# Attention with split heads and a shrink MLP: the first tile transposed in fp32, ranks computed behind tile 1, flags by another ring, copies on ScalarE

## The chip, the cores and the metric

The kernel runs on one core of a Trainium2 chip. The core has TensorE (matmuls, written PE in the profile, with its weight loads as PEld), VectorE (DVE), ScalarE (ACT), GpSimd (POOL) and SyncE (SP). SP, ScalarE and GpSimd can issue DMA transfers. All engines run in parallel, each executes its own queue in order, and they wait for each other by semaphores. The metric is the device time of one execution in microseconds (us). Lower is better.

## The reference

```python
def _attn_ref(q, k, v, is_retrieval, n_sink, window):     # q, k, v: 4 x 8 heads x 768 x 64, fp32
    scores = scale * np.matmul(q, k.transpose(0, 1, 3, 2))
    causal = rel >= 0
    stream_keep = causal & (is_sink | in_win)             # first 4 keys, or the last 64
    mask = np.where(retr[0, :, 0, 0, None, None], full_mask, stream_mask)
    ...                                                   # softmax of the masked scores
    return np.matmul(a, v)

def _moe_ref(x, w_in, w_out):                             # x: 3072 x 512, w_in 512 x 2048, w_out 2048 x 512
    h = x @ w_in
    g = h - np.tanh(h)
    return g @ w_out
```

Each of the 8 heads is either a retrieval head (causal attention over all keys) or a streaming head (the first 4 keys and a window of 64). The flags `is_retrieval` say which; 3 of 8 are set. The heads of a token side by side make the 512 columns of x.

## The kernel before, in words

**Tiles and units.** The 3072 tokens are cut into 12 tiles of 256 tokens; three tiles make one batch entry. A tile has four attention units, one for each pair of heads, so unit n belongs to tile n // 4. A unit goes through: T (TensorE transposes of q and k, `st_T`, and copies of the results from PSUM into `qT` and `kz`), S (scores, exp on ScalarE, mask product on VectorE, `st_S`), A (product with v, then a reciprocal and a product on VectorE that give x, `st_A`), X (TensorE transposes x, and a copy puts it into `xT`, `st_X`). When a tile has its four units, H units multiply xT with w_in into a `ph` bank, ScalarE takes tanh, VectorE makes `gt` (L1110), and O groups multiply gt with w_out. There are two `ph` banks, two banks pairs ("sc") shared by scores and transposes, and one bank each for A and O.

**Loads.** SP loads q, k and v in fp32 into six raw tiles used in turn (L297), so the raw q tile of tile 0 is used again by tile 2. Tile 0 is loaded in halves of four heads. The weights are loaded by GpSimd with a cast (L309, L321). Before anything else SP loads the flags (L344).

**Casts.** For tile 0 ScalarE casts three halves of q and k to fp16, VectorE the fourth (`cast_qk`, L566 and L568). GpSimd casts v. For tile 1 ScalarE casts q and k, for tile 2 GpSimd does.

**Ranks.** From tile 3 on (the second batch entry) the heads are taken in an order in which retrieval heads come first, so that the other half can use cheaper near scores. `by_rank` computes this order on VectorE by some 17 small operations, each of which uses the one before (L464 to L547), loads it into registers of GpSimd and VectorE (L553), and makes the thresholds `thrr` from which `masks` builds the masks of the ranked tiles. GpSimd then casts q, k and v of tile 3 and later by rank (`cast_ranked`, L627), and DMA transposes on SP take the place of T and X (L644, L1043). `load_count` (L1289) loads the number of set flags into a register of all five engines; after the last tile it decides whether the program must be run again without ranks (with more than 4 set flags; here it isn't).

**Order.** The program is written as a list of operations with the engine, an assumed duration, what is read and written, and optionally another operation that must come before (`after`). A planner (`Plan.run`) plays these through with the assumed durations: each engine takes, of what is ready, the operation that stands first in the list. The order found is written into the engines' queues and is fixed then. `slot` and the plan after it say between which H units the steps of the next tile's units stand in the list. In the list `by_rank` stands ahead of the first H unit, and the planner issues it as soon as VectorE is free and the flags are there. The count's load waits, in the planner's view, for the count alone.

Of the kernel before, what the change touches and what calls it, by code (L numbers as in the profile page):

```python
# [149 lines left out]
def kernel(  # L150
# [63 lines left out]
    ones = const.tile([128, 128], FP16, name="ones")  # L214
    warm = const.tile([128, 1], FP32, name="warm")
    ident16 = const.tile([128, 128], FP16, name="ident16")
    A4 = const.tile([128, 4, 128], FP16, name="A4")
    sinks = const.tile([128, 128], FP16, name="sinks")
    nz = const.tile([128, 2 * H], FP32, name="nz")
# [29 lines left out]
    def program(first):  # L249
# [90 lines left out]

        if first:
            op(
                "SP", 400,
                lambda: nc.sync.dma_start(  # L344
                    out=retr_i[:], in_=is_retrieval.bitcast(I32).partition_broadcast(128)
                ),
                w=["retr"], dma=(128, 20.0),
            )
# [3 lines left out]
        if first:  # L352

            op("POOL", 204, lambda: nc.gpsimd.memset(ones[:], 1.0), w=["ones"])
            op(
                "ACT", 1400,
                lambda: nc.scalar.activation(out=warm[:], in_=ones[:, 0:1], func=AF.Exp),
                r=["ones"], w=["warm"],
            )

            if fast:
                op(
                    "POOL", 300,
                    lambda: nc.gpsimd.affine_select(
                        out=upto[:], in_=ones[:, 0 : H * H].rearrange("p (a c) -> p a c", a=H),
                        compare_op=ALU.is_ge, fill=0.0, base=0, pattern=[[1, H], [-1, H]],
                        channel_multiplier=0,
                    ),
                    r=["ones"], w=["upto"],
                )  # L370

            def select(m, src, fill, base, step, mult, key, cmp=ALU.is_ge):
                op(
                    "POOL", 300,
                    lambda: nc.gpsimd.affine_select(
                        out=m, in_=src, compare_op=cmp, fill=fill,
                        base=base, pattern=[[step, 128]], channel_multiplier=mult,
                    ),
                    r=["ones", key], w=[key],
                )  # L380


            select(ident16[:], ones[:], 0.0, 0, 1, -1, "ident", ALU.is_equal)
            select(A4[:, 2, :], ones[:], 0.5, window_i - 1, -1, 1, "A4")
            select(sinks[:], ones[:], 0.5, n_sink_i - 1, 0, -1, "sinks")
            op(
                "DVE", 220,
                lambda: nc.vector.tensor_max(out=A4[:, 0, :], in0=A4[:, 2, :], in1=sinks[:]),
                r=["A4", "sinks"], w=["A40"],
            )  # L390
            select(A4[:, 2, :], A4[:, 2, :], 0.0, 0, 1, -1, "A4")
            select(A4[:, 3, :], ones[:], 0.5, -(128 - window_i + 1), -1, 1, "A43")
            op(
                "DVE", 220,
                lambda: nc.vector.tensor_max(out=A4[:, 1, :], in0=A4[:, 3, :], in1=sinks[:]),
                r=["A43", "sinks"], w=["A41"],
            )
# [29 lines left out]
            def make_rflag0():  # L427

                nc.vector.scalar_tensor_tensor(
                    out=rflag0[:], in0=sinks[:, 0:1].to_broadcast([128, H]), scalar=0.75,  # L430
                    in1=rflag[:], op0=ALU.is_ge, op1=ALU.max,
                )

            op("DVE", 165, make_rflag0, r=["sinks", "rflag"], w=["rflag0"])
# [19 lines left out]
        def ranked(t):  # L454
            return first and fast and t >= NG

        def by_rank():

            def dve(ns, fn, r, w):
                op("DVE", ns, fn, r=r, w=w)  # L460

            one = iota[:].unsqueeze(1).to_broadcast([128, H, H])
            dve(
# [76 lines left out]
                    out=mS[:].rearrange("p a c -> p (a c)")[:, 0:384], in0=A[:, 0:384],  # L540
                    scalar1=0.75, scalar2=None, op0=ALU.is_ge,
                ),
                r=["A4", "A40", "A41", "A43"], w=["mS"], port=True,
            )
            op(
                "DVE", 150,
                lambda: nc.vector.tensor_copy(out=mS[:, 4, :], in_=mS[:, 2, :]),  # L547
                r=["mS3"], w=["mS"], port=True,
            )
            for e, et in (("POOL", Engine.Pool), ("DVE", Engine.DVE)):  # L550

# [43 lines left out]
        def cast_ranked(t):  # L595
# [39 lines left out]
            for nm in "kq":  # L635
                for i in range(NB):
                    c0 = (g * NB + i) * KS

                    def turn(nm=nm, i=i, c0=c0):
# [8 lines left out]
                    op(  # L648
                        "SP", 1250, turn,
                        r=[key for half in range(2) for key in t16_keys(nm, t, half)],  # L650
                        w=[("kz", b % 2, g, i) if nm == "k" else ("qT", t, "all", i)],
                        dma=(128 * (8 if nm == "k" else 4), 22.0),
                    )
            if g == 0:
                for p_ in range(HP // 2):

                    def repeat(p_=p_):
# [8 lines left out]

                    hp = 2 * p_ + 1
                    op(
                        "POOL", 580, repeat, r=[("kz", b % 2, 0, 0)],
                        w=[("sinks", b % 2, hp)], port=True,  # L670
                    )

# [5 lines left out]
        def k_keys(t, hp, g):  # L678
            s = t // NG % 2
            if ranked(t):  # L680
                return [("kz", s, g, i) for i in range(NB)]
            return [("kz", s, hp, g)]

        def q_of(t, hp):
# [91 lines left out]
        def st_T(n, eq="DVE", ek=("DVE", "DVE")):  # L776
            t, hp = divmod(n, HP)
            b, g = divmod(t, NG)
            tp, key = bank([128, 2, 8, 128], FP16, "sc", f"tp{n}")
            keys = [(*key, x) for x in range(2)]  # L780
            if hp == 0:
                qT[t] = lazy(qt_pool, [128, HP, TT], FP16, "qT", f"qT{t}")
            cq, ck = t16s["q", t], t16s["k", t]

            def mm():
                for x, c in enumerate((cq, ck)):
                    for i in range(NB):
                        nc.tensor.transpose(
                            out=tp()[:, x, i, :], in_=c()[:, i, 2 * hp : 2 * hp + 2, :],
                            identity=ident16[:],  # L790
                        )

            op(
                "PE", 224, mm,
                r=["ident"] + [
                    key for nm in "qk" for key in t16_keys(nm, t, hp * 2 // HP)
                ],
                w=keys,
            )

            cost = {"ACT": 373, "DVE": 288}
            kk = kz[b % 2][:, 2 * hp : 2 * hp + 2, :]
# [380 lines left out]
        def slot(n):  # L1183
# [4 lines left out]
                res.append(qs.pop(0))  # L1188
            by_tile = ranked(n // HP)
            if n % HP and not by_tile:  # L1190
                res.append(lambda: st_X(n - 1))
            res.append(lambda: st_A(n, 0))
            if qs:
                res.append(qs.pop(0))
            res.append(lambda: st_A(n, 1))
            res += qs
            if n + 2 < NU and not ranked((n + 2) // HP):
                res.append(lambda: st_T(n + 2))
            if n % HP == HP - 1:
                if by_tile:  # L1200
                    res.append(lambda: st_X_tile(n // HP))
                else:
                    res.append(lambda: st_X(n))
            return res

        for b in range(2):
            ones_v(b)
        cast_qk(0, (("ACT", "ACT"), ("ACT", "DVE")), (0,))
        load(1, halves=range(2))
        for n in (0, 1):  # L1210
            st_T(n, "ACT", ("DVE", "DVE"))
            for f in scores(n):
                f()
        cast_v(0, ("POOL", "POOL"), (0,))
        cast_qk(0, (("ACT", "ACT"), ("DVE", "DVE")), (1,))
        for n in (0, 1):
            st_A(n, 0)
            st_A(n, 1)
# [18 lines left out]
        if first:  # L1237
            for j in range(4):
                load_w_out(j, [("win", 3)])
            if not fast:  # L1240
                for hp in range(HP):
                    zero_kz("POOL", 1, hp, 0, S, [("wout", 3)])
            if fast:
                by_rank()


        PIECES = (
# [10 lines left out]
        for t in range(1, NTT):  # L1258
# [4 lines left out]
            for hp in range(HP):  # L1263
                if t + 2 < NTT:
# [3 lines left out]
                        )  # L1268
                        for nm, i in PIECES[hp]
                    ]  # L1270
                if first and fast and t == NG - 1 and hp == HP - 1:
                    fs.append(lambda: masks(thrr, "thrr", NGEN))
                if hp == 0 and t + 1 < NTT:
                    if ranked(t + 1):
                        fs.append(lambda t=t: cast_ranked(t + 1))
                        fs.append(lambda t=t: spread_v(t + 1))
# [8 lines left out]
        if first and fast:  # L1285

            def load_count():
# [5 lines left out]
                )  # L1293

            plan[6 * NFU] = plan.get(6 * NFU, []) + [
                lambda: op("DVE", 400, load_count, r=["count"])
            ]

        def expect_skip(after, *engines):
# [71 lines left out]
```

## Time and profile before

| | |
|---|---|
| median of 5 runs | 251.59 us (250.66 to 252.67) |
| profiled execution | 251.74 us, its span 250.0 us |
| TensorE busy | 227.0 us, 91% of the span |
| VectorE, ScalarE, GpSimd busy | 151.0, 143.2, 96.4 us |
| DMA | 39.25 MB, mean 157 GB/s |

The profile shows one execution. A line of the timeline or of the groups names the engine, the line of the kernel, the operation and what it writes from what; brackets hold the idle time of the engine before it and what ended that time. The page cuts the span into 40 slices, with a digit for the tenths of it that an engine was busy. Queue entries with a q (SPq, ACTq) are what an engine's sequencer does itself, such as issuing a DMA or loading a register.

### The profile page before, as it was taken

How to read it: one execution, taken by the hardware profiler on the slowest of the kernel's cores; microseconds unless marked ns; L12 is line 12 of the kernel's file. 1: busy time of each engine (PE TensorE's matmuls, PEld its weight loads, DVE VectorE, ACT ScalarE, POOL GpSimd, SP SyncE). 2: the span in 40 equal slices, each digit the busy share in tenths (PEclk: the TensorE clock that was granted, in tenths of full speed). 3: DMA queues.
4: the chain of work that ended last, by engine and by line, in shares of the span. 5: the costliest groups of instructions: out<-in, count | busy, mean ns of one | idle time of the engine just before them, and what ended most of it. 6: DMA issues, size and time to landing. Idle time of an engine off the chain costs nothing. (4 is left out here: it accounts for less than half of the span.)

```text
span 250.0 us, 6087 instructions
## 1 busy us (share of the span) xinstructions
PE 227.0 (91%) x2204; PEld 167.0 (67%) x2204; DVE 151.0 (60%) x375; ACT 143.2 (57%) x215; POOL 96.4 (39%) x286
## 2 busy tenths in 40 slices
PE   0259999999999899999999899999999999999992
PEld 0146876786677578776777577776777777666661
DVE  7686786774468637666686555567676454643410
ACT  3357864876367539655386555547667566433430
POOL 5146080139954815937447088364340000000000
PEclk9999999999999999999999999999999999999999
DMA  5999999999979989999899999998981211041121
GB/s 124 209 201 195 197 211 188 221 204 215 201 152 210 160 173 239 184 245 194 165 210 197 184 213 153 232 138 172 220 164 64 51 45 42 5 84 42 45 81 52
DMA packets 121667, 39.25 MB, mean 157 GB/s; under 512 B 114336, under 2 KB 118688, under 8 KB 121632
## 3 DMA queue, kind: packets, MB, share of 16 engines
q1 hardware_dynamic: 117264, 34.49, 71.2%
q0 software_dynamic: 4224, 4.19, 10.1%
q8 instruction: 18, 0.29, 0.5%
q14 instruction: 17, 0.14, 0.2%
q10 hardware_dynamic: 144, 0.13, 0.2%
HBM read 27.27 MB, written 6.29 MB: 134 GB/s over the span
## 5 line engine op out<-in xcount | busy, mean ns | idle before, releaser
L1090 PE MATMUL ph<-xT,win 128*128 128x256 f16 x768 | 99.0, 273 | 1.2 <-DVE gt L1110 0.7
L1149 PE MATMUL po<-wout,gt 128*128 128x512 f16 (+1 forms) x400 | 98.1, 370 | 0.9 <-ACT ot L1125 0.9
L1110 DVE SCALAR_TENSOR_TENSOR gt<-th,ph 128x512 f16<-128x512 f32 x96 | 65.8, 685 | 53.4 <-ACT th L1103 53.2
L1103 ACT ACTIVATE th<-ph 128x512 f32<-128x512 f32 x96 | 57.4, 598 | 64.9 <-PE ph L1090 62.9
L1090 PEld LDWEIGHTS <-win 128*128 128x128 f16 x768 | 72.2, 98 | 16.8 <-issue 1.2
L936 ACT ACTIVATE pt<-sc 128x768 f16<-128x768 f32 (+1 forms) x60 | 53.9, 917 | 16.1 <-PE sc L918 15.6
L1149 PEld LDWEIGHTS <-gt 128*128 128x128 f16 x400 | 36.7, 98 | 24.0 <-issue 1.3
L918 PE MATMUL sc<-qT,kz 128*128 128x256 f16 (+1 forms) x280 | 34.7, 259 | 5.2 <-DVE kz L774 3.2
L985 PEld LDWEIGHTS <-pt 128*128 128x128 f16 x552 | 26.4, 99 | 12.0 <-DVE pt L949 2.0
L627 POOL CAST k<-raw_k 128x128 f16 x72 | 20.0, 321 | 31.6 <-DMA raw_k<-in_k_dram 24.9
L918 PEld LDWEIGHTS <-kz 128*128 128x128 f16 x280 | 24.2, 102 | 11.5 <-DVE kz L774 3.7
L985 PE MATMUL av<-v,pt 128*128 128x65 f16 x304 | 26.0, 198 | 1.5 <-DVE pt L949 1.5
L627 POOL CAST t_q<-raw_q 128x128 f16 x72 | 19.7, 313 | 16.9 <-DMA raw_q<-in_q_dram 16.5
L1015 DVE TENSOR_TENSOR x16t<-av,rinv 128x128 f32 x72 | 20.9, 290 | 2.2
L627 POOL CAST v<-raw_v 128x128 f16 x72 | 19.3, 312 | 6.0 <-DMA raw_v<-in_v_dram 5.9
L985 PE MATMUL av<-vf,pt 128*128 128x65 f16 x248 | 20.0, 193 | 0.5 <-ACT pt L936 0.5
L875 ACT ACTIVATE pt<-sc 128x1024 f16<-128x1024 f32 (+1 forms) x18 | 17.2, 954 | 4.2 <-PE sc L861 3.3
L1125 ACT ACTIVATE ot<-po 128x512 f32<-128x512 f32 (+1 forms) x24 | 14.2, 593 | 9.0 <-PE po L1149 8.7
L954 DVE TENSOR_TENSOR pt<-pt,m 128x1024 f16<-128x1024 f16 x20 | 14.5, 726 | 4.2 <-ACT pt L936 3.9
L1005 DVE RECIPROCAL rinv<-av 128x4 f32<-128x4 f32 x48 | 8.6, 179 | 12.6 <-PE av L985 11.9
L892 DVE TENSOR_TENSOR pt<-pt,mS 128x512 f16<-128x512 f16 x24 | 10.7, 485 | 6.7 <-ACT pt L875 6.7
L568 POOL CAST v<-raw_v 128x512 f16<-128x512 f32 x6 | 4.0, 673 | 19.2 <-DMA raw_v<-in_v_dram 16.2
(71 smaller groups left out, 122.4 us busy)
## 6 DMA issues: line engine op xcount, KB each, us to landing
out_dram<-ot SPq DMA_DIRECT2D x23, 256.0 KB, 2.5
raw_q<-in_q_dram SPq DMA_DIRECT2D x20, 256.0 KB, 4.6
raw_k<-in_k_dram SPq DMA_DIRECT2D x20, 256.0 KB, 4.2
raw_v<-in_v_dram SPq DMA_DIRECT2D x20, 256.0 KB, 5.0
win<-in_moe_w_in_dram POOLq DMA_DIRECT2D x4, 512.0 KB, 10.2
wout<-in_moe_w_out_dram POOLq DMA_DIRECT2D x4, 512.0 KB, 11.7
raw_q<-in_q_dram SPq DMA_DIRECT2D x8, 128.0 KB, 3.2
raw_k<-in_k_dram SPq DMA_DIRECT2D x8, 128.0 KB, 3.3
```

Of the source, the lines that this page charges most:

```text
L627: nc.gpsimd.tensor_copy(out=o, in_=r()[:, :, at, :])
L875: lambda: nc.scalar.activation(out=pt()[:, :, 0:wid], in_=sc()[:, :, 0:wid], func=AF.Exp, scale=inv_sqrt_d),
L918: nc.tensor.matmul(out=sc()[:, hh, o : o + nb * 128], lhsT=kk[:, hh, jb * KS : jb * KS + 128], rhs=q_of(t, hp)[:, q0 * 128 : (q0 + nb) * 128],
L936: lambda: nc.scalar.activation(out=pt()[:, :, 512 * gi : 512 * gi + wid], in_=sc()[:, :, 0:wid], func=AF.Exp, scale=inv_sqrt_d,),
L954: nc.vector.tensor_mul(out=pv, in0=pv, in1=m4[:, hs, 256:512].unsqueeze(2).to_broadcast([128, 2, 2, 256]),)
L985: nc.tensor.matmul(out=av()[:, i, hh, :], lhsT=pt()[:, hh, co : co + 128], rhs=vv, start=(jb == first_jb), stop=(jb == qb),)
L1015: nc.vector.tensor_mul(out=x16s[t]()[:, :, at, :], in0=av()[:, :, hh : hh + 1, 0:D], in1=rinv()[:, :, hh : hh + 1].unsqueeze(3).to_broadca ...
L1090: nc.tensor.matmul(out=ph()[:, j, :], lhsT=w_in_t[fb // 4]()[:, cb, f0 : f0 + 128], rhs=xTs[t]()[:, cb, :], start=(cb == 0), stop=(cb == H ...
L1103: lambda: nc.scalar.activation(out=th()[:], in_=ph()[:], func=AF.Tanh, scale=1.0 / XS),
L1110: lambda: nc.vector.scalar_tensor_tensor(out=gts[t]()[:, u * FU : (u + 1) * FU, :], in0=th()[:], scalar=-XS, in1=ph()[:], op0=ALU.mult, op ...
L1125: nc.scalar.activation(out=ot()[:, c0:c1], in_=po()[:, c0:c1], func=AF.Copy, scale=1.0 / XS)
L1149: nc.tensor.matmul(out=po()[:, c0:c1], lhsT=gts[t]()[:, f, ts * 128 : ts * 128 + 128], rhs=w_out_t[f // 4]()[:, f % 4, c0:c1], start=(f == ...
```

## The change

For tile 0, q and k are no longer cast. `st_T` transposes the fp32 raw tiles directly, with an fp32 identity, into fp32 PSUM; the copies out of PSUM write fp16 as before. The identity is one more select on GpSimd. In `st_T` the transposes of q and of k become two operations of the list instead of one. `by_rank` moves into tile 2: each of its VectorE operations but the two register loads gets the first unit's scores of tile 2 as an operation that must come before. The ranked casts of tile 3 move one unit later in the list. The flags are loaded by ScalarE's DMA queue. The copies of `st_X` in tiles 1 and 2, and those of q in `st_T` for units 6 to 11, move from VectorE to ScalarE. The count's load is put behind the first gt of tile 4. Keys of the planner for the ranked k get a part "all", which keeps them apart from those of unranked units.

```diff
+    ident32 = const.tile([128, 128], FP32, name="ident32")
...
             op(
-                "SP", 400,
-                lambda: nc.sync.dma_start(
+                "ACT", 400,
+                lambda: nc.scalar.dma_start(
                     out=retr_i[:], in_=is_retrieval.bitcast(I32).partition_broadcast(128)
...
+            select(ident32[:], ones[:], 0.0, 0, 1, -1, "ident32", ALU.is_equal)
             select(ident16[:], ones[:], 0.0, 0, 1, -1, "ident", ALU.is_equal)
...
-        def by_rank():
+        def by_rank(after):
 
             def dve(ns, fn, r, w):
-                op("DVE", ns, fn, r=r, w=w)
+                op("DVE", ns, fn, r=r, w=w, after=after)
...
-                        w=[("kz", b % 2, g, i) if nm == "k" else ("qT", t, "all", i)],
+                        w=[("kz", b % 2, "all", g, i) if nm == "k" else ("qT", t, "all", i)],
...
-            tp, key = bank([128, 2, 8, 128], FP16, "sc", f"tp{n}")
+            dt, ident, ns = (FP32, ident32, 440) if t == 0 else (FP16, ident16, 112)
+            tp, key = bank([128, 2, 16 // mybir.dt.size(dt), 128], dt, "sc", f"tp{n}")
...
+            def turn(x, c):
+                for i in range(NB):
+                    nc.tensor.transpose(
+                        out=tp()[:, x, i, :], in_=c()[:, i, 2 * hp : 2 * hp + 2, :],
+                        identity=ident[:],
+                    )
+
+            for x, nm in enumerate("qk"):
+                if t == 0:
+                    c, slot = raws[nm, t]
+                    r = [("raw", slot, i, hp * 2 // HP) for i in range(NB)] + ["ident32"]
+                else:
+                    c, r = t16s[nm, t], t16_keys(nm, t, hp * 2 // HP) + ["ident"]
+                op("PE", ns, lambda x=x, c=c: turn(x, c), r=r, w=keys[x : x + 1])
...
-                res.append(lambda: st_X(n - 1))
+                res.append(lambda: st_X(n - 1, eng="ACT"))
...
-                res.append(lambda: st_T(n + 2))
+                res.append(lambda: st_T(n + 2, "ACT"))
...
-                    res.append(lambda: st_X(n))
+                    res.append(lambda: st_X(n, eng="ACT"))
...
-        cast_qk(0, (("ACT", "ACT"), ("ACT", "DVE")), (0,))
...
-        cast_qk(0, (("ACT", "ACT"), ("DVE", "DVE")), (1,))
...
-            if fast:
-                by_rank()
...
+                if first and fast and (t, hp) == (2, 0):
+                    fs.append(lambda n=t * HP + hp: by_rank(first_S[n]))
                 if first and fast and t == NG - 1 and hp == HP - 1:
                     fs.append(lambda: masks(thrr, "thrr", NGEN))
-                if hp == 0 and t + 1 < NTT:
+                if hp == (1 if t == NG - 1 else 0) and t + 1 < NTT:
...
-                lambda: op("DVE", 400, load_count, r=["count"])
+                lambda: op("DVE", 400, load_count, r=["count", ("gt", 4, 0)])
```

More of the change, by code (lines that the diff above doesn't have):

```diff
@@ L542, in by_rank @@
                 ),
-                r=["A4", "A40", "A41", "A43"], w=["mS"], port=True,
+                r=["A4", "A40", "A41", "A43"], w=["mS"], port=True, after=after,
             )
@@ L547, in by_rank @@
                 lambda: nc.vector.tensor_copy(out=mS[:, 4, :], in_=mS[:, 2, :]),
-                r=["mS3"], w=["mS"], port=True,
+                r=["mS3"], w=["mS"], port=True, after=after,
             )
@@ L668, in cast_ranked @@
                     op(
-                        "POOL", 580, repeat, r=[("kz", b % 2, 0, 0)],
+                        "POOL", 580, repeat, r=[("kz", b % 2, "all", 0, 0)],
                         w=[("sinks", b % 2, hp)], port=True,
@@ L680, in k_keys @@
             if ranked(t):
-                return [("kz", s, g, i) for i in range(NB)]
+                return [("kz", s, "all", g, i) for i in range(NB)]
             return [("kz", s, hp, g)]
@@ L782, in st_T @@
                 qT[t] = lazy(qt_pool, [128, HP, TT], FP16, "qT", f"qT{t}")
[L783 to L799, printed above, removed]
+            def turn(x, c):
[11 more added lines that the diff above has]
+                op("PE", ns, lambda x=x, c=c: turn(x, c), r=r, w=keys[x : x + 1])
             cost = {"ACT": 373, "DVE": 288}
```

## The prediction

> **What bounds the kernel now.** I began with the page's slices (6.25 us each), to see where TensorE is idle.
>
> ```profile
> PE   0259999999999899999999899999999999999992
> ...
> DVE  7686786774468637666686555567676454643410
> ACT  3357864876367539655386555547667566433430
> ```
>
> From the fourth slice on TensorE is at 9; it lost time in the first three and at the very end. So a saving counts where it shortens the start, and a cost counts where it stops TensorE after about 20 us. By stretches, TensorE is busy 6.96 of the first 20 us (13.04 idle) and idle for only some 5 us from there to 240. The chain of work that ended last names only the final VectorE copy, so the waits of TensorE in the first 25 us came next:
>
> ```profile
> PE tp L788 <- ACT t_q L566: 5.3, 1, 5.3
> PE sc L918 <- DVE kz L774: 2.9, 2, 2.6
> PE xp L1063 <- DVE x L1029: 1.7, 1, 1.7
> PE av L985 <- DVE pt L949: 1.5, 1, 1.5
> PE tp L788 <- ACT k L566: 1.1, 1, 1.1
> ```
>
> Each is one hop of a latency chain. Then the timeline of that chain (start, duration, engine, line, operation, idle before and releaser):
>
> ```profile
> 1.37 0.97 SPq L297 DMA_DIRECT2D raw_q<-in_q_dram  x2
> ...
> 6.12 0.62 ACT L566 CAST k<-raw_k 128x512 f16<-128x512 f32 x1 [0.83 <-DMA raw_k<-in_k_dram]
> ...
> 6.80 0.40 PE L788 MATMUL tp<-ident,k 128*128 128x128 f16 x2 [1.06 <-ACT k L566]
> ...
> 8.27 0.37 ACT L772 COPY qT<-tp 128x256 f16<-128x256 f16 x1 [1.53 <-DVE pos_a L490]
> ...
> 8.91 0.28 DVE L774 COPY kz<-tp 64x256 f16<-64x256 f16 x1 [0.44 <-ACT qT L772]
> ...
> 9.75 0.80 PE L918 MATMUL sc<-qT,kz 128*128 128x256 f16 x4 [2.56 <-DVE kz L774]
> ```
>
> k has been transposed at 7.20, yet ScalarE copies q at 8.27. The instructions of the register load of the count show why (engine, operation, duration in ns, start):
>
> ```profile
> L1289 SPq TENSOR_LOAD <-count_i x1: 472/472/472, 7.7 to 7.7; - x1
> L1289 ACTq TENSOR_LOAD <-count_i x1: 475/475/475, 7.7 to 7.7; - x1
> ...
> L1289 PEldq TENSOR_LOAD <-count_i x1: 487/487/487, 9.2 to 9.2; - x1
> ```
>
> Every engine waits in its queue for the count and then loads it; ScalarE stands from 6.74 to 8.27 and SP loses 0.79 us in the middle of its load issues (two issues took 1.84 us, not 1.05). Last, a table of stretches for VectorE and ScalarE later (length, busy PE, PEld, DVE, ACT, POOL, clock, DMA):
>
> ```profile
> 20.00:32.00 12.00, 11.04 (x122) 8.88 (x119) 9.43 (x26) 9.53 (x15) 4.11 (x6) 1.00 1.22 197
> 44.00:52.00 8.00, 8.00 (x83) 6.43 (x82) 5.92 (x16) 6.61 (x10) 1.84 (x5) 1.00 1.11 206
> ```
>
> **The Trainium skill.** "TensorE: Matmul & The Clock Gate", Terms, says the transpose mode is 4x faster for FP32; under "Weight-path perf modes" it says that the fast weight load is off for FP32. So fp32 transposes need not cost four passes, but may load weights more slowly; the trace of before has only fp16 ones (a pair takes 0.39 to 0.42 us at the start, 0.27 from 26 us on). "DMA: Bandwidth & Descriptors", "Issuing engines are not separate DMA queues", says that another issuing engine saves only sequencer time; the trace agrees, the flags' issue holds SP 0.40 us. The same page, "Latency and other measured facts", gives a register load a floor of about 600 ns; here it is 0.47 to 0.62.
>
> **The change, part by part.**
>
> *Flags by ScalarE's ring.* q's first load is issued at 0.91 instead of 1.37: q and k of tile 0 land 0.46 us earlier. On ScalarE one issue of 0.40 stands before the table load (0.89 to 2.17) and nothing there is wanted before 4.68. The flags landed 2.6 us after issue; VectorE read them at 4.19, behind its memsets. No cost.
>
> *No cast of tile 0.* Gone are three casts on ScalarE (0.62, 0.62, 0.63) and one on VectorE (0.43). k was seen at 6.12, so now at 5.66; its transposes follow at once. The extra identity is one more select of 0.25 on POOL, before 3.2 us, when VectorE's readers are still behind memsets: nothing. The price of 16 fp32 transposes isn't in the trace. Low end: as fp16, 0.105 apart at this stage, nothing extra. High end: four passes, 0.42 each, 16 x 0.315 = 5.0 us more. I take twice, 0.21 (slower weight load), 1.7 us more in all, in a stretch where TensorE is busy 6.17 of 12 us (8 to 20).
>
> *Ranks and count out of the start.* VectorE loses 17 small operations there (0.51 + 1.06 + 0.21 + 0.69 = 2.5 us by the timeline), the 0.62 load of the ranks and the 0.56 of the count, ScalarE its 1.53 of standing, SP its 0.79. With 0.46 + 0.79 all loads from the last of tile 0 on are up to 1.25 us earlier.
>
> *The new start.* The eight masks on VectorE need POOL's selects, done at 5.04, so they run 5.1 to 7.3 (2.18 as now). The q copy on ScalarE is done by then and k is in PSUM at 6.1 to 6.6, so the two kz copies take 7.3 to 7.9 and the first scores start at 8.0 instead of 9.75 (-1.75). Next unit: scores to exp 0.84, exp 0.81, then on VectorE mask 0.54 and two copies 0.57, 0.1 of hops: a cycle of 2.85, where the trace has 3.07, 2.42 and 3.75. Second scores 10.85 (12.82), third 13.7 (15.24), fourth 16.55 (18.99; there one kz copy stood behind a scaling, a mask and a product until 18.43, and VectorE is now 2.9 us freer). **-2.4 us** at the fourth unit, and through its normalised x at the first win matmul (26.24 to 23.8). Tile 2's q may be loaded only once the fourth unit's transposes have read the raw tile (about 15.4); its issue is at 15.79 now.
>
> *What the earlier start meets.* Landings of win are 22.9, 26.4, 29.9, 33.1 against first uses 26.24, 29.50, 33.38, 35.94: slack 2.8 to 3.5. Those of wout are 39.7, 43.0, 46.5, 49.8 against 43.37, 45.77, 49.59, 52.99: 2.7 to 3.7. All exceed 2.4, and POOL issues them after casts and transposes that move forward too. Hidden.
>
> *Copies to ScalarE in tiles 1 and 2.* Six q and eight x copies: VectorE -14 x 0.29 = -4.1, ScalarE +14 x 0.371 = +5.2. In 20 to 32 us four of them make ScalarE 9.53 + 1.48 = 11.0 of 12, VectorE 9.43 - 1.16 = 8.3. One engine is relieved, the other filled: between -0.3 and +1.5; I take nothing.
>
> *Ranks at tile 2.* In 44 to 52 VectorE is busy 5.92 of 8. Two q copies leave (-0.58), 2.5 + 0.62 come: 8.46 of 8, so **+0.45** on a full TensorE. Queued behind are the gt products (L1110), which free the ph banks that TensorE waits for, and kz copies. Low end 0; high end, the 17 run as one dependent chain at the 0.26 spacing seen at 9.68, 9.94, 10.20: 4.4 + 0.62 = 5.0, less 0.7 that two ph banks cover (a unit each 2.0 us, minus tanh 0.6 and product 0.7): 4.3. POOL waits for the ranks too, but its ranked casts wait for tile 3's q until 51.34 anyway. Casting tile 3 one slot later is hidden by the same wait.
>
> *Count at tile 4* (first product there about 91 to 98 us). Each engine loads once: TensorE 0.49, ScalarE 0.48, VectorE 0.56. TensorE's queue is 64 deep (the skill's TensorE page, "Architectural detail"; no trace here shows it), so most should be covered: **+0.1**, ends 0 and 0.6. SP and POOL have waits there anyway (POOL 7.8 us for raw_k before 96.36).
>
> Renamed keys and the split of a transpose operation in two add no instruction.
>
> Sum: -2.4 + 0.45 + 0.1 = -1.85. The profiled execution took 251.74 (span 250.0 and 1.74 around it): 249.9. It is 0.15 above the median 251.59, so about **249.7**.
>
> **Rivals.** *Bigger gain* (0.15): kz copies slip in between masks (first scores at 7.0) and the later costs vanish: 251.6 - 3.3 = 248.3. *Partly taken back* (0.22): either fp32 costs four passes, so units 2 to 4 wait for transposes (1.7 us each; scores at 11.1, 14.25, 17.4, gain 1.6, with the costs above 250.5), or ScalarE becomes the bound of tile 1 and takes back 1.5 (251.2): exps of 1.02 stand before copies that scores and win matmuls wait for. For it: 11.0 of 12. Against: VectorE was as full. Middle 250.9. That transfers eat the gain is part of this; the slacks speak against. *Slower* (0.18): the rank chain at tile 2, unbroken: 4.3 + 0.5 for the count - 2.4 = +2.4, 254.0. It decides once TensorE idles 3.7 us more than now in 40 to 56. For it: VectorE is overfull there by the sum, and TensorE has nothing spare. Against: independent masks and copies can fill the chain's gaps.
>
> **Numbers.** Likeliest (0.45): 249.7, its own range 248.6 to 250.8, about 1.1 each way, since a list scheduler writes every queue's order and each moved operation can reshuffle what follows it. About 0.5%, 1.26 us, is what a measurement can tell: faster is below 250.33, slower above 252.85. Faster: 0.36 of the likeliest, 0.15, and 0.02 of the third, 0.53. Same: 0.09 + 0.20 = 0.29. Slower 0.18. The range 248.0 to 253.0 leaves out most of the slower case and a little below.
>
> **What would show it.** First scores near 8.0, fourth near 16.6, first win matmul near 23.8; fp32 pairs at 0.4 to 0.5 us (0.9 or more: four passes); no idle of TensorE beyond 0.5 us at the ranks and none at the count. I am wrong if the masks or the flags hold up kz copies longer, if tile 1's scores wait for ScalarE, or if products at tile 2 come late.

## The result, and the profile after

The changed kernel takes 253.07 us (median of 29 runs, 250.63 to 255.0) against 251.56 for the kernel before in the same job (50 runs). Some executions fall into a slower state, three of the changed kernel's here, and the ratios below are formed without them: 1.0048, 95% interval [1.0032, 1.0064]. It is slower by half a per cent; 249.7 was predicted. Its profiled execution took 252.74 us, its span is 251.0.

The page's row of TensorE after (40 slices of 6.3 us, tenths busy):

```profile
PE   2667989999999999999999999999999999999992
```

TensorE is busier in the first three slices (2, 6, 6 for 0, 2, 5), partly because it starts earlier and partly because the same work takes it longer: its busy time over the whole span grew from 227.0 to 231.5 us, and 3.1 of these 4.5 us fall in the first 25 us (94 matmuls in 14.5 us, 95 in 11.4 before). By stretches, its idle time up to 25 us fell from 13.6 to 10.5 us, and from there to 240 us from 4.5 to 4.0. The 3.6 us less of waiting are outweighed by 4.5 us more of matmuls. The waits of TensorE in the first 25 us (total, times, longest):

```profile
PE tp L790 <- DMA raw_q<-in_q_dram: 4.3, 1, 4.3
PE av L987 <- DVE pt L951: 2.5, 3, 1.2
PE sc L920 <- DVE kz L776: 1.9, 2, 1.6
```

TensorE now waits for the load itself and no longer for the casts (5.3 and 1.1 us before), less for kz (2.9) and more for a mask product (1.5). The timeline of the first two units after (start, duration, engine, line, operation, idle before and its releaser):

```profile
5.36 2.31 DVE L443 TENSOR_SCALAR m<-A,thr 128x512 f16<-128x512 f16 x8 [0.44 <-POOL A L376]
...
7.59 0.87 DVE L776 CAST kz<-tp 64x256 f16<-64x256 f32 x2
...
8.05 0.96 PE L920 MATMUL sc<-qT,kz 128*128 128x256 f16 x4 [1.55 <-DVE kz L776]
...
8.80 0.63 PE L790 MATMUL tp<-ident,raw_q 128*128 128x128 f32 x2
...
9.05 0.81 ACT L938 ACTIVATE pt<-sc 128x768 f16<-128x768 f32 x1 [3.35 <-PE sc L920]
9.23 0.63 PE L790 MATMUL tp<-ident,raw_k 128*128 128x128 f32 x2
...
9.89 0.56 DVE L951 TENSOR_TENSOR pt<-pt,m 128x768 f16<-128x768 f16 x1 [1.44 <-ACT pt L938]
...
10.48 0.88 DVE L776 CAST kz<-tp 64x256 f16<-64x256 f32 x2
...
10.95 0.96 PE L920 MATMUL sc<-qT,kz 128*128 128x256 f16 x4
```

The first scores start at 8.05 and the second at 10.95, as predicted (8.0 and 10.85). The third start at 14.47 (predicted 13.7), the fourth at 17.66 (16.55), and the first win matmul is at 26.52 instead of 23.8. All of the gain is gone there (26.24 before). Of the 2.7 us that are missing, 1.1 were lost up to the fourth scores and 1.6 behind them. From the first win matmul to the last group of output matmuls (238.11 after, 237.16 before) it takes 0.7 us longer than before, which is near the 0.55 that the prediction allowed for ranks and count. What the operations on the transposed blocks cost is in the view by tile (count: duration in ns, least/median/most, first and last start):

```profile
L790 PE MATMUL tp<-ident,raw_q x8: 417/421/475, 4.3 to 15.3; 128*128 128x128 f32 x8
...
L776 DVE CAST kz<-tp x8: 408/422/430, 7.6 to 17.6; 64x256 f16<-64x256 f32 x8
L790 PE MATMUL tp<-ident,t_q x6: 264/312/314, 18.4 to 26.2; 128*128 128x128 f16 x6
...
L776 DVE COPY kz<-tp x6: 272/288/295, 19.3 to 27.8; 64x256 f16<-64x256 f16 x6
```

An fp32 pair starts 0.43 us after the one before (8.80 and 9.23), an fp16 pair 0.21 (10.35 and 10.56 before). The copy of k out of fp32 PSUM takes 0.42 instead of 0.29. The later stretches (length, then busy PE, PEld, DVE, ACT, POOL):

```profile
20.00:32.00 12.00, 10.60 (x103) 8.33 (x103) 7.60 (x16) 8.19 (x14) 2.48 (x3) 1.00 1.22 204
44.00:52.00 8.00, 7.87 (x70) 5.84 (x68) 6.77 (x28) 7.38 (x12) 0.43 (x1) 1.00 1.22 214
```

Around the ranks (44 to 52) TensorE is idle for 0.13 us only, so they aren't what costs there. In 20 to 32 it holds 103 matmuls, where before had 122.

### The profile page after: what moved, and what is told of

The parts are those of the page before. It is cut to its first block, busy times and chain, and to the rows that moved or that the text cites. A ratio compares the mean times of both kernels' runs of the same rounds, so it can differ in the third digit from the quotient of the medians.

```text
span 251.0 us, 6086 instructions
## 1 busy us (share of the span) xinstructions
PE 231.5 (92%) x2204; PEld 168.9 (67%) x2204; DVE 149.3 (59%) x360; ACT 145.4 (58%) x226; POOL 98.0 (39%) x287
## 5 line engine op out<-in xcount | busy, mean ns | idle before, releaser
L1092 PE MATMUL ph<-xT,win 128*128 128x256 f16 x768 | 100.7, 274 | 0.6 <-DVE gt L1112 0.4
L920 PEld LDWEIGHTS <-kz 128*128 128x128 f16 x280 | 23.6, 102 | 9.4 <-DVE kz L776 3.3
L629 POOL CAST t_q<-raw_q 128x128 f16 x72 | 19.4, 309 | 13.2 <-DMA raw_q<-in_q_dram 12.8
L629 POOL CAST v<-raw_v 128x128 f16 x72 | 20.0, 321 | 7.9 <-DMA raw_v<-in_v_dram 7.8
```

What stands on the lines that cost most here:

```text
L629: nc.gpsimd.tensor_copy(out=o, in_=r()[:, :, at, :])
L920: nc.tensor.matmul(out=sc()[:, hh, o : o + nb * 128], lhsT=kk[:, hh, jb * KS : jb * KS + 128], rhs=q_of(t, hp)[:, q0 * 128 : (q0 + nb) * 128],
L1092: nc.tensor.matmul(out=ph()[:, j, :], lhsT=w_in_t[fb // 4]()[:, cb, f0 : f0 + 128], rhs=xTs[t]()[:, cb, :], start=(cb == 0), stop=(cb == H ...
```

## The experiments

All kernels together; the ratio is to the kernel before, run in the same job. "Re-planned": the planner orders the changed list. "Old order": the list of before is planned, and the edits are made as its operations are issued.

| run | what it has of the change | ratio | 95% interval |
|---|---|---|---|
| after | all | 1.0048 | 1.0032 to 1.0064 |
| e1_start | fp32 start, flags' ring | 1.0053 | 1.0028 to 1.0078 |
| e2_ranks | ranks and count | 1.0014 | 0.9994 to 1.0034 |
| e3_copies | copies on ScalarE | 1.0042 | 1.0023 to 1.0061 |
| e4_start_ranks | all but the copies | 1.0216 | 1.0176 to 1.0256 |
| e5_all_old_order | all, old order | 1.0259 | 1.0232 to 1.0287 |
| e6_ranks_old_order | ranks and count, old order | 1.0196 | 1.0166 to 1.0226 |
| e7_start_old_order | start, old order | 1.0104 | 1.0071 to 1.0137 |
| e8_copies_old_order | copies, old order | 1.0108 | 1.0066 to 1.0150 |
| e9_null_plan_a | nothing, other plan | 1.0018 | 0.9995 to 1.0041 |
| e10_null_plan_b | nothing, other plan | 1.0025 | 1.0003 to 1.0047 |
| e11_ranks_v_first | e2_ranks, one load issued sooner | 1.0046 | 1.0024 to 1.0068 |
| e12_warm_old_order | nothing, 84 matmuls added | 1.0010 | 0.9988 to 1.0032 |
| e13_light_before | nothing, lighter loads | 1.0066 | 1.0043 to 1.0089 |
| e14_light_ranks | e2_ranks, lighter loads | 1.0144 | 1.0111 to 1.0178 |
| e15_light_after | all, lighter loads | 1.0023 | 1.0008 to 1.0038 |
| e16_ranks_copies | ranks, count, copies | 0.9978 | 0.9963 to 0.9994 |
| e17_fp16_at_fp32_price | e16 with fp32's price | 1.0134 | 1.0094 to 1.0173 |
| e18_all_but_fp32 | all but fp32 | 0.9957 | 0.9934 to 0.9980 |

### The parts alone

From the changed kernel, what a run doesn't have is put back as it was:

```diff
# without the start
-  op("ACT", 400, lambda: nc.scalar.dma_start(out=retr_i[:], ...
+  op("SP", 400, lambda: nc.sync.dma_start(out=retr_i[:], ...
-  dt, ident, ns = (FP32, ident32, 440) if t == 0 else (FP16, ident16, 112)
+  cast_qk(0, (("ACT", "ACT"), ("ACT", "DVE")), (0,))       # and the second half
# without the ranks
-  if first and fast and (t, hp) == (2, 0): fs.append(lambda n=...: by_rank(first_S[n]))
+  if fast: by_rank(None)                                     # ahead of the first H unit
-  lambda: op("DVE", 400, load_count, r=["count", ("gt", 4, 0)])
+  lambda: op("DVE", 400, load_count, r=["count"])
# without the copies
-  st_X(n - 1, eng="ACT"); st_T(n + 2, "ACT"); st_X(n, eng="ACT")
+  st_X(n - 1); st_T(n + 2); st_X(n)
```

> Only the new start: fp32 transposes of tile 0, no casts, flags by ScalarE's ring; ranks, count and copies stay as before. Theory A (the copies on ScalarE in tiles 1 and 2 lose the time): the first scores come only near 8.9, since the count's load still holds ScalarE and VectorE works on the ranks; the time is 0.3 to 1.0 us below before. Theory B (the start itself loses it, since VectorE's mask meets GpSimd's scaling at 20 to 22 us and TensorE's pace doubles only near 29 us instead of 25): at least 0.7 us above before, with pairs of fp16 transposes still 0.42 us at 26 us. Theory C (ranks at tile 2): no slower than before.

> Only ranks and the count's load moved, with tile 3's ranked casts a unit later. Theory A and B: 0 to 1 us below before, since ScalarE's stand of 1.5 us at 6.7 to 8.3 is gone. Theory C: 1 us or more above before, with TensorE idle by over 1 us more than before in 40 to 60 us.

> Only the x copies and the q copies of units 6 to 11 on ScalarE. Theory A: 1 to 2.5 us above before, the seventh and eighth scores (28.0 and 31.6 before) 1 to 2 us later, TensorE waiting for VectorE's x or kz. Theory B and C: within 0.7 us of before.

> The whole change without the copies on ScalarE. Theory A: 1 to 2 us below before (249.6 to 250.6), first scores at 8.0 and the eighth at or before 31.6. Theory B: like after (252.5 to 253.5), with the late doubling of TensorE's pace. Theory C: 0.5 to 1.5 us above before.

The start alone costs 0.5% and the copies alone 0.4%; the ranks alone change nothing that can be told. The parts don't add up: start and ranks together are 2.2% slower, which none of the three theories foresaw, and adding the copies to them brings it back to 0.5%.

In e1_start, where the ranks stay in the start, the first win matmul is at 25.16 us, 1.1 us earlier than before, and TensorE's pace doubles near 22 us, not 29 as theory B had it (weight loads that follow each other at once stand 0.106 us apart up to there and about 0.055 later). The loss comes behind that: the last group of output matmuls starts at 237.48, 0.3 us later than before. What takes these 1.4 us isn't known.

In e2_ranks the first scores start at 8.0 us and the first win matmul at 23.72. So the ranks alone bring the whole gain of the start that I had worked out for the change, with the casts in place. It is lost later. These are the waits of TensorE at 40 to 62 us and at 105 to 200 us (total, times, longest), in an execution of 252.85 us, 1.1 above the median of this kernel:

```profile
PE av L986 <- POOL v L568: 1.1, 1, 1.1
...
PE ph L1091 <- DMA xT<-x16t: 1.9, 1, 1.9
```

The first wait is the price of the new place: GpSimd's cast of v stands in its queue behind the register load of the ranks. In e4_start_ranks the wait for xT is 3.5 us in two pieces. In e3_copies the copy of q on ScalarE stands behind a tanh, VectorE waits for it, and the x product behind comes late. TensorE waits 1.04 us for that x, and so it does in the changed kernel (at 33.92, also 1.04):

```profile
31.64 0.42 ACT L772 COPY qT<-tp 128x256 f16<-128x256 f16 x1
...
32.09 0.28 DVE L774 COPY kz<-tp 64x256 f16<-64x256 f16 x1 [0.65 <-ACT qT L772]
...
33.36 0.28 PE L1064 MATMUL xp<-ident,x 128*128 128x128 f16 x2 [1.04 <-DVE x L1030]
```

### The order of before kept

Since the planner may place everything anew, the same parts were put into the order of before.

```diff
+  # ranks: taken out of the planned order, put back from tile 2's first scores on,
+  # two behind each VectorE operation; the count behind the first gt of tile 4
+  out += group[:2]; group = group[2:]
+  # start: casts of tile 0 issue nothing; transposes read the raw tile with ident32
+  if gone: op(e, cost, lambda: None, r=r, w=w)
+  # copies: the engine is changed as the copy is issued
+  copy("ACT" if n >= 6 else eq, qT[t]() ...
```

> All edits of the change, but every queue keeps the order that the planner wrote for the kernel before: casts of tile 0 are left out at their places, transposes, flags and copies change their engine or type in place, the rank operations stand two at a time behind VectorE's operations after the first scores of tile 2, the count behind the first product of tile 4. Theory O (the other orders that the planner writes lose the gain of the start): 249.5 to 250.8, a gain of 0.7 to 2. Theory D (loads, GpSimd's casts and DMA transposes keep their pace, so that an earlier TensorE waits in later tiles whatever the order): 251.0 to 252.0. Theory A (the copies on ScalarE cost by themselves): 252 to 253.

> Only ranks and count moved, in the order of before. Theory O: 249.0 to 250.3 with the first win matmul near 23.8 and the last matmul 1.3 to 2.5 us earlier. Theory D: 251.2 to 252, the first win matmul just as early, but waits of TensorE for DMA transposes or GpSimd's casts of 1.5 us or more in all after 45 us.

> Only the fp32 start and the flags' ring, in the order of before, ranks and count at the start. Theory O: 250.8 to 251.6 (first scores at 9 to 9.5, where the count's load still stands in ScalarE's queue). Theory D: the same as before within 0.4. If fp32 transposes are a loss by themselves: above 252.

> Only the copies on ScalarE, in the order of before. Theory A: 252.3 to 253.3, with TensorE waiting over 1 us for VectorE's x or kz at 30 to 35 us. Theory O and D: 251 to 252.

Every part measured slower in the old order than re-planned, though for the start the two intervals overlap. So nothing here supports the theory that the planner's new orders lose a gain that the edits have. It isn't refuted either: the old order was planned for other work, and the place of the ranks in it was chosen by hand. e5 and e6 came out slower than any theory had it. In e7 the first win matmul is at 27.87 us, 1.6 later than before, and 1.8 us are missing at the last group of output matmuls. In e6 the ranks show what they can cost when they stand densely. A table of stretches of TensorE (length, busy, granted clock, DMA):

```profile
46.00:48.00 2.00, 0.00 (x0) 0.81 1.21 251
48.00:50.00 2.00, 1.51 (x10) 0.50 0.81 179
50.00:55.00 5.00, 5.00 (x28) 0.59 1.15 226
```

VectorE runs ranks, register load and masks until 47.66, kz comes at 47.85, and TensorE waits 3.5 us for it in all. Then its clock is at 0.5 to 0.6 for seven microseconds. Between the middle of tile 1's H and the start of tile 2's this kernel goes from 2.2 us ahead of before to 4.2 behind. That is my rival for the slower side, with about the idle time from which I said it decides; the changed kernel itself doesn't have it.

### The plan alone, one issue, and a busy TensorE

```diff
-  op("PE", 224, mm,                                # e9: the planner's price of a transposed pair
+  op("PE", 236, mm,
-  cost = {"ACT": 373, "DVE": 288}                  # e10: its price of a copy
+  cost = {"ACT": 373, "DVE": 300}
+  order.insert(order.index(vload[0]) + 1, vload[1])  # e11, on e2_ranks: tile 11's V
+  fill(30 | 26 | 10 | 6 | 12)                      # e12: matmuls of ones into an unused bank
```

> No work is changed: the planner is told that a pair of fp16 transposes lasts 236 ns in place of 224, and re-orders the list from about tile 2 on. If the time of this kernel follows from its work, it is that of before within 0.3% (250.8 to 252.3). If the planned order alone carries some per cent, it lies outside: 0.4% or more away, on either side, and the order is then a cause of its own for what the parts of the change showed.

> No work is changed: the planner is told that VectorE's copy of a transposed block lasts 300 ns in place of 288, and re-orders the list from the fourth unit on. Work alone: within 0.3% of before (250.8 to 252.3). Order as a cause of its own: 0.4% or more away, on either side, and not the same figure as the other kernel whose plan alone is changed.

> The ranks alone are moved, as in e2_ranks, and on SyncE one issue is put two places earlier: the second block of V of tile 11 goes directly behind the first, ahead of the transposed k that waits for GpSimd's casts. Theory that the early gain was lost to the order of SyncE's in-order queue: the wait of 1.9 us for xT at tile 8 goes, and the time is 249.3 to 250.4, 0.5 to 0.9% below before. Rival, that the gain is lost to something that grows back in any order (GpSimd's casts or the transfers are late by themselves): 251.4 to 252.2, with the wait elsewhere.

> The kernel before in its own order, with 84 matmuls 128x128 on a bank that nobody reads put between TensorE's first instructions, so that it is never idle for long from 2 to 18 us. If TensorE's half pace until about 25 us costs time there: weight loads stand 0.055 us apart from 10 us on in place of 0.106, the first win matmul moves from 26.2 to 24 to 25 us, and the end by as much where the gain is carried: 249.4 to 250.6. If VectorE, ScalarE and the loads set the pace of the start: H of tile 0 starts within 0.5 us of 26.2 and the time is within 0.3% of before. If the added matmuls stand before work that waits: 252 to 253.

These two new plans with no change of work moved the time by about 0.2%, less than any part that was found to cost, and about as much as e16 gains below. e11 didn't bring the gain that its theory asked for: the wait for xT is gone from 150 to 200 us, but TensorE idles 2.3 us at 100 to 150, where e2_ranks has 0.3, and this lies ahead of the issue that was moved. So a single trace can't place losses of 2 us there, and the order of SyncE's queue isn't shown to be what took the gain. Nor is it known why e4 loses 2%.

e12 changed nothing either, and its trace, of an execution 1.7 us above the median, shows two things that stood against it: 26 added matmuls stood before the first scores (10.97 instead of 9.75), and the fast pace, there from about 14 us on, didn't last. Its stretches (length, busy, granted clock, DMA):

```profile
15.00:20.00 5.00, 2.90 (x46) 1.00 1.00 185
20.00:25.00 5.00, 4.02 (x31) 0.50 1.22 197
```

It did help while it lasted: from the first scores to the fourth took 8.1 us instead of 9.2. A version that keeps TensorE busy to 25 us without standing in the way was not tried.

### Lighter loads

```diff
-  in_=src[b, h0 : h0 + nh, s0 : s0 + 128, :].rearrange("h p d -> p h d")
+  in_=src[b].rearrange("h s d -> (h s) d")[n * 1024 : (n + 1) * 1024, :]   # from tile 2 on
+      .rearrange("(p h) d -> p h d", h=nh)
```

> The kernel before, but from tile 2 on q, k and v are loaded as contiguous pieces of the same size (2 KB for each partition in place of eight pieces of 256 bytes), so other data are computed on; the work and its order stay. It is the base for the next two. If transfers are what holds the middle of the kernel, the DMA row leaves 9 after 30 us, TensorE's idle time from 25 to 240 us falls from 4.1 us to 1 or 2, and the time is 248 to 250. If not: within 0.3% of before.

> e2_ranks with the same lighter loads. Theory that saturated transfers take the early gain of 2.5 us back: with light loads it is carried, and this kernel is 1.5 to 2.5 us (0.6 to 1.0%) below e13_light_before. Rival, that it is given back to waits between engines and to TensorE's own busy time: within 0.3% of e13_light_before, as e2_ranks is of before.

> The changed kernel with the same lighter loads. Transfers as the cause: 0.5 to 2 us below e13_light_before, since its first scores are 1.7 us earlier. Rival, that the fp32 start, the late doubling of TensorE's pace and the copies on ScalarE cost by themselves: 0.3 to 0.8% above e13_light_before, as the changed kernel is above before.

The base itself got slower, so the three can't tell what they were made for. The waits for xT and qT of the middle are gone, and the loads land sooner (median 3.8 us for 4.6 for q), but the weights land later, and GpSimd issues the last two win transfers from 22.1 us on instead of 19.1. This is TensorE's wait for win in e13, and the time of the four win transfers from issue to landing there (least/median/most; 7.2/10.2/13.2 before), in an execution 2.0 us above the median:

```profile
PE ph L1094 <- DMA win<-in_moe_w_in_dram: 3.8, 2, 2.8
...
DMA to landing us min/median/max: 7.6/12.6/16.8
```

In e14, where the first win matmul is wanted soonest, it waits 4.2 us for win. The changed kernel, whose H starts late anyway, waits 0.4 us for it in e15. In these runs an earlier TensorE runs into the transfers of the weights.

### Without fp32, and with its price alone

```diff
# e16: the changed kernel without the start.  e18: e16 with the flags on ScalarE's ring
# e17: e16 with, in tile 0,
-  for i in range(NB):
+  for i in (0, 0, 1, 1) if t == 0 else range(NB):          # each transpose twice
+  if t == 0: copy(ek[hh], dst[:, lo : lo + 1, 0:128], ...)  # one block of k once more
```

> Ranks and copies as in the changed kernel, but tile 0 cast to fp16 as before and the flags by SyncE. If the parts act for themselves, the sum of e2_ranks (+0.1%) and e3_copies (+0.4%): 252.4 to 253.2. If the fp32 start is what costs in the changed kernel: 250.5 to 251.8. If each plan brings a figure of its own: outside 251.5 to 253.5.

> The list of e16_ranks_copies, in which tile 0 is cast to fp16 and no order changes, with the price of fp32 put in: each transpose of tile 0 is issued twice (a pair then takes 0.42 us of TensorE from start to start, as an fp32 pair does) and behind each of its copies of k VectorE copies one block once more (0.28 and about 0.18 us, for the 0.43 us of a copy from fp32). If the price of fp32 in the start is what the changed kernel loses against e16_ranks_copies: units of tile 0 about 3.1 us apart in place of 2.7, first win matmul near 25.5 to 26.5 in place of 23.5, time 252.2 to 253.2. If the plan or the later tiles are what it loses: 250.3 to 251.2, as e16_ranks_copies.

> The whole change but for fp32: ranks, copies and the flags by ScalarE's ring; tile 0 is cast to fp16 as before. If the ring of the flags is worth its 0.46 us of earlier loads, the first scores start 0.2 to 0.5 us before the 8.0 of e16_ranks_copies and the time is 250.0 to 250.6. If VectorE's masks, which end near 7.6 us, set the first scores, they start within 0.15 us of 8.0 and the time is that of e16_ranks_copies within 0.3%. If fp32 is not what costs in the changed kernel: 252 or more.

e18 is 0.43% faster than before, and its interval and that of the changed kernel don't meet. All that sets them apart is fp32 in tile 0 and the plan that goes with it: 0.9%, 2.3 us. e17 keeps the plan of e16 and shows that such a price in the start is carried to the end: twice the transposes and half a copy more turn 0.2% faster into 1.3% slower. Its first win matmul is at 27.97 instead of 23.48, and the last group of output matmuls at 240.67 instead of 235.65. It isn't a measure of what the changed kernel pays. It is slower than expected (255.46 us, not 252.2 to 253.2): it keeps the casts, its two copies take 1.12 us, not 0.87, and in the order of e16 the q copy of the second unit stands behind the k copies. How much of the 0.9% is the price of fp32 and how much the other plan isn't separated. The timeline of the second unit of e17:

```profile
9.37 0.63 PE L789 MATMUL tp<-ident,t_q 128*128 128x128 f16 x4
...
10.47 1.12 DVE L774 COPY kz<-tp 64x256 f16<-64x256 f16 x4 [1.45 <-PE tp L789]
...
12.11 0.80 PE L920 MATMUL sc<-qT,kz 128*128 128x256 f16 x4 [1.67 <-ACT qT L772]
```

The timeline of the start of e18, and the one place where it waits for win:

```profile
6.02 0.62 ACT L566 CAST k<-raw_k 128x512 f16<-128x512 f32 x1 [0.55 <-DMA raw_k<-in_k_dram]
...
7.13 0.37 ACT L772 COPY qT<-tp 128x256 f16<-128x256 f16 x1 [0.49 <-PE tp L789]
...
7.53 0.61 DVE L774 COPY kz<-tp 64x256 f16<-64x256 f16 x2
...
7.87 0.82 PE L919 MATMUL sc<-qT,kz 128*128 128x256 f16 x4 [0.78 <-DVE kz L774]
...
8.49 0.42 PE L789 MATMUL tp<-ident,t_q 128*128 128x128 f16 x2
...
9.16 0.61 DVE L774 COPY kz<-tp 64x256 f16<-64x256 f16 x2 [1.02 <-PE tp L789]
...
9.80 0.56 DVE L950 TENSOR_TENSOR pt<-pt,m 128x768 f16<-128x768 f16 x1
...
10.28 0.80 PE L919 MATMUL sc<-qT,kz 128*128 128x256 f16 x4 [1.16 <-ACT qT L772]
...
27.13 1.05 PE L1091 MATMUL ph<-xT,win 128*128 128x256 f16 x8 [0.94 <-DMA win<-in_moe_w_in_dram]
```

The transposes of e17 take 0.63 us for 0.42, the copies 1.12 for 0.6, and the second scores come at 12.11, not at 10.28. With casts e18 has its first scores at 7.87, earlier than the changed kernel without them (8.05). k is cast at 6.64, q is copied by 7.50, and kz is copied at 7.53; VectorE's masks are done at 7.39. From there scores follow at 2.4, 2.7 and 3.0 us, against 2.9, 3.5 and 3.2 after. First win matmul: 23.40 against 26.52.

## Why the prediction was wrong

**No cast of tile 0** is the step that failed. Its price per fp32 transpose was right (0.21 taken, 0.21 measured), but it was left out of the sum, on the ground that TensorE is idle half of that stretch. The two kz copies were kept at 0.57, as from fp16 PSUM; from fp32 they took 0.87. So fp32 stood in the sum with no cost at all. The kernels that differ in this step and its plan alone are after and e18: fourth scores at 17.66 against 15.97, first win matmul at 26.52 against 23.40. e4 and e2, which differ in the flags' ring too, give 17.50 against 16.09, and 24.63 against 23.72.

The timelines show how the price gets in. In e18 the transposes of the second unit end at 9.13, while the exp still runs (8.74 to 9.55), and both kz copies are done ahead of the mask (9.80). After, the fp32 transposes end at 9.86, just when the exp does, and the planner's order has the mask first and the copies behind it. This is the chain that the prediction worked out as 2.85 us, and it took 2.90; e18 needs only 2.41. That the first two scores came out as forecast is in part luck: the masks end 0.3 us later than forecast (near 7.6) and the copies are wider, but the scores start behind the first of the two copies, and not behind both. In the third unit (3.52 us, 2.66 in e18) the first kz copy waits for the q copy on ScalarE too, and the second, wider one stands behind the mask. The timeline of the third unit after, and of the fourth unit's mask:

```profile
12.80 0.37 ACT L774 CAST qT<-tp 128x256 f16<-128x256 f32 x1
...
13.21 0.42 DVE L776 CAST kz<-tp 64x256 f16<-64x256 f32 x1 [1.18 <-ACT qT L774]
...
13.55 0.54 DVE L951 TENSOR_TENSOR pt<-pt,m 128x768 f16<-128x768 f16 x1
14.12 0.43 DVE L776 CAST kz<-tp 64x256 f16<-64x256 f32 x1
...
19.93 1.66 DVE L951 TENSOR_TENSOR pt<-pt,m 128x768 f16<-128x768 f16 x1
...
20.09 2.40 POOL L759 TENSOR_TENSOR vf<-v,rflag 128x520 f16<-128x520 f16 x2
...
21.64 0.51 PE L987 MATMUL av<-v,pt 128*128 128x65 f16 x6 [0.66 <-DVE pt L951]
```

Whether another order of copies and mask would have saved some of it was not tried.

The other side of the step earned nothing. With the ranks gone, the chain through the casts is ready about when the masks are: in e18 the q copy, its last link, ends at 7.50 and the masks at 7.39. So e18, which keeps the casts, starts its scores no later. After, the masks begin only at 5.36, at 5.08 in e18, since VectorE does its first product on A, for which GpSimd waits, at 4.42 instead of 4.21; whether the added identity brought that isn't shown.

**Ranks and count out of the start** was right: first scores 8.0 in e2_ranks and e16. The whole of the -2.4 at the first win matmul belongs to this step (-2.5 in e2_ranks, -2.8 in e18).

**What the earlier start meets** was wrong by about a microsecond. The slack of win was read from landings and uses before, and GpSimd's issues were said to move forward too. In e18 TensorE is 2.8 us earlier, but GpSimd's first win issue is at 16.02 (15.74 before), and TensorE waits 0.94 us for win at 27.13. Half way through tile 0's H the gain of e18 is 1.5 us (31.84 for 33.38), and at the last group of output matmuls 0.8. The measured gain of e18 is 1.1 us, not 1.85.

**From the fourth unit to the first win matmul** the prediction carried its -2.4 us over unchanged. This stretch took 7.25 us before and 7.43 in e18, but 8.86 after, which is 1.6 of the missing 2.7 us. fp32 alone doesn't bring it: e4 has the same fp32 start and takes 7.13. The 65 matmuls of this stretch are busy for 7.32 us after, for 6.38 before and 6.04 in e18; TensorE is idle for 1.54, 0.87 and 1.39 us. Of the idle time after, 0.66 is the wait for the fourth unit's mask (shown above): it takes 1.66 us while GpSimd scales v, where the same mask in e4 starts 0.17 us earlier and takes 0.61. As to the busy time, the doubling of TensorE's pace comes near 25 us before, near 20 in e18, near 23 in e4, and near 29 after, so the first 16 win matmuls take 1.91 us before and in e18, and 2.82 after. Why it comes so late after, and what the collision with GpSimd is worth, wasn't tested. The Trainium skill, "TensorE: Matmul & The Clock Gate", Part 1 (the clock gate), ties the doubling to about 3.4 us of sustained activity; TensorE is busy 4.08 of 5 us at 15 to 20 in e18 and 3.95 after, which doesn't tell the two apart.

**Copies to ScalarE**, taken as nothing between -0.3 and +1.5: alone they cost 1.1 us (e3, the mechanism of the rival, an x that comes 1.04 us late); beside the ranks they don't cost (e16 against e2_ranks, whose intervals just touch), and beside ranks and start they gain (after against e4).

**Ranks at tile 2**, +0.45: 0.13 us of idle TensorE in 44 to 52. VectorE was busy 6.77 there, not 8.46, and the planner put the small operations between others (45.8 to 50.6). **The count**, +0.1: TensorE idles 0.32 us in 100 to 125, 0.17 before.

**Flags by ScalarE's ring**: the first load is issued 0.46 us earlier, as predicted, but it didn't land as much earlier. k's loads take 3.7 us to land in e18 and 3.4 in e16 (medians), the cast of k starts at 6.02 for 6.11, and the first scores gain 0.09 (7.87 for 7.96).

The rivals: *partly taken back* named fp32 but only with four passes, and fell short of the loss. *Slower* named the ranks, which is what e6 does and the changed kernel doesn't. Of the signs that were named, the first scores, the fp32 pairs and TensorE at the ranks came out as forecast; the fourth scores and the first win matmul didn't.

## What to carry to other kernels

In a start where every unit is one chain across engines, idle time of an engine is no room for a longer operation: ask what stands behind it. Here transposes that end 0.4 us later against the exp left no room for the copies ahead of the mask. Price a changed type at each reader and writer of the block, the copy out of PSUM included. When several waits are removed at once, ask which one ends last after the others are gone; here the casts held up the first scores by 0.1 us at most once the ranks were moved. Of a gain at the start, count only what the next limits leave over, such as the weights' transfers in e18.

## What was not expected of the hardware

- A 64x256 copy on VectorE from PSUM takes 0.42 us from fp32 and 0.29 from fp16. A 128x128 transpose at the slow pace comes every 0.21 us in fp32 and every 0.106 in fp16.
- TensorE loses its fast pace quickly. In e6, 3.2 us without a matmul were followed by a granted clock of 0.50 to 0.59 until 55 us; in e12, a stretch of 5 us with 2.1 us of idle time was followed by 0.50. The clock row of the profile shows 1.00 before the first doubling, though weight loads are 0.106 us apart there: the pace of the start is read from the loads, not from that row.
- Loads in pieces of 2 KB instead of 256 bytes made the kernel slower by 0.66% (e13). They land sooner (q after 3.8 us instead of 4.6, medians), and the weights, in another queue, land later (12.6 instead of 10.2).
- The fourth unit's mask product on VectorE (128x768, fp16) takes 0.56 us in e18, ahead of GpSimd's scaling of v. Where it runs beside that scaling it takes 0.98 (before), 1.17 (e1), 1.33 (e17) and 1.66 us (after).
